# An opening reordered: two row blocks of w_in loaded and multiplied ahead of batch 0's last head pair, seven columns open instead of six

## The chip, the cores and the metric

The kernel runs on one core of one Trainium2 chip. The metric is device microseconds of that core for one launch. Before the change it takes 258.86 us, the median of 3 runs (258.49 to 258.88).

## What is computed

For 8 batches, 8 heads, 576 positions and head size 64, a linear attention is followed by an RMS norm per head, and its output, put side by side over the heads, goes through a two-layer block with a quick GELU:

```python
kv  = einsum('bhsd,bhse->bhde', k, v)
out = einsum('bhsd,bhde->bhse', q, kv)
x   = out / sqrt(mean(out * out, -1) + 1e-6) * g_norm      # then heads side by side: 4608 x 512
h   = x @ w_in                                              # w_in 512 x 2048
g   = h * (1 / (1 + exp(-1.702 * h)))
y   = g @ w_out                                             # w_out 2048 x 512
```

Inputs and output are float32 in memory; the loads cast to float16 and products are summed in float32.

## The kernel before, in words

The 4608 rows are worked in nine tiles of 512: tile t (0 to 7) holds the first 512 positions of batch t, and the ninth the 64 positions left over of each batch. The hidden size 2048 is 16 columns of 128 (`fo`), and the model size 512 is four row blocks of 128 (`ko`); row block c of w_in meets x of head pair c, since two heads of 64 make 128. A hidden column is four TensorE matmuls of 128x512 that add up in one PSUM bank, one for each row block. Below, (k, f) is the matmul of row block k into column f (`Hidden.mm`, line 478).

Tiles 1 to 8 use a seven-product scheme for both layers (lines 589 and 709). Tile 0, with which the program opens, is done plainly: hidden columns at line 478, the second layer at line 822 (`project_all`). Everything is issued in the order in which the code is written (`manual_schedule`), each engine works through its own list, and semaphores are set by the framework.

The opening, lines 860 to 923, works through the four head pairs c of batch 0. For each of them:

- `kv(c)`: 12 small matmuls (line 261) give k'v, and VectorE writes it into `kvb` (line 429);
- `q(c)`: 12 transposes (line 439) turn q, and VectorE copies them to `qT` (line 445);
- `out(c)`: one matmul (line 307) gives `outT`, ScalarE squares it into `sq` (line 325);
- `ss(c)`: one matmul with ones (line 384) sums the squares, ScalarE makes the reciprocal root `rs` (line 386);
- `apply(c)`: VectorE multiplies `outT`, g and `rs` into block c of `xT` (line 394), which is the x of row block c.

`busy(n)` (line 869) issues n matmuls of 128x512 whose result nobody reads. Columns are opened as the x blocks come: before the change six of them, in the order of `COLS`, get row blocks 0 to 2 and then, in one sweep, row block 3 and their activation `gate` (line 487). The ten that are left follow one at a time in `first_columns` (line 804), each with four matmuls and a gate. A column holds a PSUM bank from its first matmul until its gate. There are three pools of banks: `ps_h` (three), `ps_a` (three) and `ps_o` (two).

All loads but pair 0's go through GpSimd's queue (POOL), in the order written: q, k and v of pairs 1 to 3 (line 91, 144 KB each), w_in in pieces (line 180), then w_out (line 206) and batch 1's q, k and v. Eight semaphores serve these loads in turn, so a load is issued only when the one eight places ahead of it has landed.

Of the kernel before, what the change touches and what calls it, by code (L numbers as in the profile page):

```python
# [7 lines left out]
F16 = mybir.dt.float16  # L8
# [4 lines left out]
P = 128  # L13
# [3 lines left out]
def kernel(  # L17
# [12 lines left out]
    B, H, S, D = q.shape  # L30
    DM = H * D
    DFF = moe_w_in.shape[1]
    NPAIR = H // 2
    FO = DFF // P
    KO = DM // P
# [6 lines left out]
    EARLY = 2  # L42
    PE_ = 96
    NJ = S // PE_
    GROUP = 6
    COLS = (0, 1, 2, 3, 8, 9, 10, 11, 4, 5, 6, 12, 13, 7, 14, 15)
    assert PE_ * NJ == S and PE_ % 32 == 0

# [7 lines left out]
    ps_a = ctx.enter_context(tc.tile_pool(name="ps_a", bufs=3, space=bass.MemoryType.PSUM))  # L56
    ps_h = ctx.enter_context(tc.tile_pool(name="ps_h", bufs=3, space=bass.MemoryType.PSUM))
    ps_o = ctx.enter_context(tc.tile_pool(name="ps_o", bufs=2, space=bass.MemoryType.PSUM))
# [31 lines left out]
    def early_load(n, b, c0, c1):  # L90
        nc.gpsimd.dma_start(  # L91
            out=raw[n][0:PE_, c0:c1, :].rearrange("p c (l x) -> p (c l) x", l=2),
            in_=early_src(n, b, c0, c1),
        )
# [84 lines left out]
    def load_w_in(f0, f1, k0=0, k1=KO):  # L179
        nc.gpsimd.dma_start(  # L180
            out=w_in_sb[:, k0:k1, f0 * P : f1 * P],
            in_=moe_w_in[k0 * P : k1 * P, f0 * P : f1 * P].rearrange(
                "(ko ki) f -> ki ko f", ki=P
            ),
        )

    for c in range(1, NPAIR):
        for n in "qkv":
            early_load(n, 0, c, c + 1)
    load_w_in(0, 4, 0, 1)  # L190
    load_w_in(0, 4, 1, 2)
    load_w_in(0, 4, 2, 3)
    load_w_in(8, 10)
    load_w_in(0, 4, 3, KO)
    load_w_in(10, 12)
    load_w_in(4, 8)
    load_w_in(12, FO)

    nc.scalar.preload_act_table_set("abs_reciprocal_sqrt_and_small")
    nc.vector.memset(eps_t, EPS)  # L200
# [220 lines left out]
    class First(Early):  # L421
# [10 lines left out]
                ones2.rearrange("p (l d) -> p l d", l=2),  # L432
            )

        def q(self, c):
            t = ps_h.tile([P, S], F16, name="q0", tag="hT")
            for j in range(NJ):
                for hl in range(2):
                    nc.tensor.transpose(
                        t[hl * D : (hl + 1) * D, j * PE_ : (j + 1) * PE_],  # L440
                        qraw[0:PE_, c, (hl * NJ + j) * D : (hl * NJ + j + 1) * D],
                        ident[0:PE_, 0:PE_],
                    )
            s = attn.tile([P, S], F16, name="qT", tag="qT", bufs=4)
            nc.vector.tensor_copy(s, t)
            self.qT[c] = s
# [340 lines left out]
    def layers(t, units1, units2):  # L787
        hid = d0 if t == 0 else Hidden(t)
        seven = Seven(t, hid.gT) if t else None
        left = hid_seven(t, hid, seven, units1) if t else first_columns(hid, units1)  # L790
        osbs[t] = opool.tile([P, 4, DM], F32, name="osb", tag="osb")
        if t:
            todo = {n: [lambda x=x: seven.sums(*x) for x in xs] for n, xs in plan(t).later.items()}
            for n, us in units2.items():
                todo.setdefault(n, []).extend(us)
            for n, us in left.items():
                todo[n] = us + todo.get(n, [])
            seven.run(todo)
        else:
            project_all(hid.gT, units2)  # L800
        if EARLY <= t < B and t not in HALVED:
            store(t, 0, J)

    def first_columns(hid, units):

        for i, fo in enumerate(COLS):
            if i >= GROUP:
                for ko in range(KO):
                    hid.mm(ko, fo)
                hid.gate(fo)  # L810
            for u in units.get(i, ()):
                u()
# [45 lines left out]
    a0 = First(0)  # L858
# [8 lines left out]
    def busy(n):  # L867
        for _ in range(n):
            nc.tensor.matmul(  # L869
                idle_ps,  # L870
                kvb[1][:, 0, :],
                kvb[1].rearrange("p c r -> p (c r)"),
                start=True,
                stop=True,
            )
# [14 lines left out]
    a0.kv(1)  # L890
    a0.ss(0)
    a0.out(1)
    a0.q(2)
    busy(1)
    a0.kv(2)
    a0.ss(1)
    a0.apply(0)
    a0.out(2)
    a0.q(3)
    a0.apply(1)  # L900
    d0 = Hidden(0)
    busy(3)
    a0.kv(3)
    a0.ss(2)
    a0.apply(2)
    d0.mm(0, 0)
    d0.mm(0, 1)
    a0.out(3)
    d0.mm(0, 2)
    d0.mm(0, 3, ps_a, "att")  # L910
    for fo in range(4):
        d0.mm(1, fo)
        if fo == 1:
            a0.ss(3)
            a0.apply(3)
    for fo in range(4):
        d0.mm(2, fo)
    for fo in COLS[4:GROUP]:
        for ko in range(KO - 1):
            d0.mm(ko, fo, ps_o, "o")  # L920
    for fo in COLS[0:GROUP]:
        d0.mm(KO - 1, fo)
        d0.gate(fo)
# [197 lines left out]
```

## Time and profile before

| what | value |
|---|---|
| median of 3 runs | 258.86 us |
| profiled execution, first to last instruction (span) | 256.5 us |
| median less that span | 2.36 us |
| PE busy / PE clock granted | 98% of the span / 1.000 |
| VectorE, ScalarE, GpSimd busy | 76%, 69%, 23% |
| first hidden matmul of tile 0 | starts at 13.81 us |
| first matmul of the second layer of tile 0 | starts at 28.23 us |

Start times are microseconds from the span's start. A row of the timeline gives start, duration, engine, line, operation, what it writes and reads, how many instructions were merged into the row, and, in brackets, how long the engine had stood idle before it and what ended that. PE is the matmul part of TensorE, PEld its weight loads, DVE VectorE, ACT ScalarE, POOL GpSimd. A matmul's duration holds its way through the array; the next one starts well before it ends, so the pace of a stretch is read from starts, not from durations. The time of a run of the profiled execution itself is not given apart from its span; what the runs take beyond the span is put down as the 2.36 us above.

### The profile page before, as it was taken

How to read it: one execution, taken by the hardware profiler on the slowest of the kernel's cores; microseconds unless marked ns; L12 is line 12 of the kernel's file. 1: busy time of each engine (PE TensorE's matmuls, PEld its weight loads, DVE VectorE, ACT ScalarE, POOL GpSimd, SP SyncE). 2: the span in 40 equal slices, each digit the busy share in tenths (PEclk: the TensorE clock that was granted, in tenths of full speed). 3: DMA queues.
4: the chain of work that ended last, by engine and by line, in shares of the span. 5: the costliest groups of instructions: out<-in, count | busy, mean ns of one | idle time of the engine just before them, and what ended most of it. 6: DMA issues, size and time to landing. Idle time of an engine off the chain costs nothing.

```text
span 256.5 us, 6359 instructions
## 1 busy us (share of the span) xinstructions
PE 250.5 (98%) x2600; PEld 203.8 (79%) x2600; DVE 194.4 (76%) x341; ACT 177.0 (69%) x322; POOL 57.8 (23%) x94
## 2 busy tenths in 40 slices
PE   7899999999999999999999999999999999999994
PEld 2444544788888888888888888888888889888883
DVE  1557585999958895989588867986899687857872
ACT  3469725978759885989598958995798569537800
POOL 8882155404080104301340143000000000000013
PEclk9999999999999999999999999999999999999999
DMA  7999999998999989998999699909500730012005
GB/s 180 189 201 205 205 204 196 191 178 128 165 183 214 118 115 172 216 273 109 211 170 137 87 228 128 177 4 156 184 4 0 93 155 3 0 75 91 3 19 146
DMA packets 68703, 35.33 MB, mean 138 GB/s; under 512 B 37986, under 2 KB 66274, under 8 KB 68418
## 3 DMA queue, kind: packets, MB, share of 16 engines
q0 software_dynamic: 37648, 18.31, 55.4%
q1 hardware_dynamic: 30624, 16.29, 28.7%
q8 instruction: 20, 0.33, 0.6%
q10 hardware_dynamic: 402, 0.33, 0.4%
q14 instruction: 9, 0.07, 0.1%
HBM read 36.70 MB, written 9.44 MB: 180 GB/s over the span
## 4 chain that ended last, share of the span: by engine, by line
PE 94%; DMA 2%; POOL 2%; DVE 0%; issue 0%
PE o L709 38%; PE h L589 38%; PE o L822 5%; PE hT L478 5%; DMA vbuf<-in_v_dram 2%; PE kvp L248 2%; PE outR L337 1%; PE ss L384 1%; POOL qraw L91 1%; PE outT L307 1%; POOL kraw L91 0%; PE q L459 0%; PE kvp L261 0%; PE idle L869 0%; PE kv L261 0%; PE outT L311 0%
## 5 line engine op out<-in xcount | busy, mean ns | idle before, releaser
L566 ACT ACTIVATE gT<-h 128x512 f16<-128x512 f32 x96 | 52.4, 602 | 5.7 <-PE h L589 5.7
L589 PEld LDWEIGHTS <-ws 128*128 128x128 f16 x512 | 50.0, 98 | 6.0
L709 PEld LDWEIGHTS <-gS 128*128 128x128 f16 x512 | 49.0, 98 | 6.2 <-DVE gS L641 0.3
L589 PE MATMUL h<-xS,ws 128*128 128x256 f16 x384 | 52.2, 273 | 0.0
L709 PE MATMUL o<-tw,gS 128*128 128x256 f16 x384 | 45.6, 273 | 0.0
L589 PEld LDWEIGHTS <-w_in_sb 128*128 128x128 f16 x384 | 37.5, 98 | 4.7
L709 PEld LDWEIGHTS <-gT 128*128 128x128 f16 x384 | 37.6, 98 | 4.3
L709 PE MATMUL o<-w_out_sb,gT 128*128 128x256 f16 x256 | 31.4, 273 | 0.0
L589 PE MATMUL h<-xT,w_in_sb 128*128 128x256 f16 x224 | 31.1, 272 | 0.0
L603 DVE TENSOR_TENSOR h<-h,s 128x512 f32<-128x512 f32 x32 | 22.3, 698 | 4.4 <-PE h L589 2.8
L605 DVE TENSOR_TENSOR s<-h,s 128x512 f32<-128x512 f32 x32 | 22.1, 691 | 4.3 <-PE h L589 3.5
L686 DVE TENSOR_TENSOR osb<-o,qf 128x512 f32<-128x512 f32 (+1 forms) x25 | 16.7, 668 | 11.2 <-PE o L709 11.1
L743 POOL DMA_DIRECT2D out_dram<-osb x6 | 3.2, 538 | 93.2 <-DVE osb L686 93.2
L641 DVE TENSOR_TENSOR gS<-gT 128x512 f16<-128x512 f16 (+2 forms) x32 | 21.3, 684 | 0.6 <-ACT gT L566 0.6
L566 ACT ACTIVATE gT<-s 128x512 f16<-128x512 f32 x32 | 19.8, 628 | 2.8 <-DVE s L605 2.8
L589 PE MATMUL h<-xS,w_in_sb 128*128 128x256 f16 x128 | 18.9, 273 | 0.0
L353 DVE TENSOR_REDUCE sum<-sq 128x8 f32<-128x512 f16 x24 | 14.9, 679 | 4.7 <-ACT sq L347 4.7
L995 ACT ACT_TABLE_LOAD x14 | 18.0, 1283 | 0.3
L535 DVE COPY s<-h 128x512 f32<-128x512 f32 x19 | 13.0, 685 | 6.5 <-PE h L589 6.4
L325 ACT ACTIVATE sq<-outT 128x512 f16<-128x512 f32 (+1 forms) x16 | 7.8, 493 | 14.3 <-PE outT L307 8.7
L115 POOL DMA_DIRECT2D kraw<-in_k_dram x7 | 6.0, 855 | 49.1 <-PE kvp L248 32.5
L386 ACT ACTIVATE rs<-ss,eps_t 128x512 f32<-128x512 f32 (+1 forms) x16 | 9.2, 581 | 11.2 <-PE ss L384 11.2
(105 smaller groups left out, 372.2 us busy)
## 6 DMA issues: line engine op xcount, KB each, us to landing
out_dram<-osb SPq DMA_DIRECT2D x8, 512.0 KB, 5.4
kraw<-in_k_dram POOLq DMA_DIRECT2D x5, 512.0 KB, 6.0
vbuf<-in_v_dram POOLq DMA_DIRECT2D x5, 512.0 KB, 10.0
out_dram<-osb SPq DMA_DIRECT2D x2, 1024.0 KB, 4.1
qraw<-in_q_dram POOLq DMA_DIRECT2D x3, 512.0 KB, 11.0
qbuf<-in_q_dram POOLq DMA_DIRECT2D x3, 512.0 KB, 12.8
out_dram<-osb SPq DMA_DIRECT2D x6, 192.0 KB, 6.7
w_in_sb<-in_moe_w_in_dram POOLq DMA_DIRECT2D x2, 512.0 KB, 9.6
```

The source lines that it names most:

```text
L353: nc.vector.tensor_reduce(out=self.sum4[:, j, :], in_=self.o[j][1].rearrange("p (x d) -> p x d", d=D), op=ALU.add, axis=mybir.AxisListType.X,)
L478: nc.tensor.matmul(self.h[fo], w_in_sb[:, ko, fo * P : (fo + 1) * P], self.x[:, ko], start=(ko == 0), stop=(ko == KO - 1),)
L535: (nc.vector.tensor_copy if engine == "D" else nc.scalar.copy)(to, src)
L566: nc.scalar.activation(self.gT[:, to, n * TH : (n + 1) * TH], src, AFT.Gelu_apprx_sigmoid)
L589: nc.tensor.matmul(bank[name][:, a], w, x, start=(p in (1, 5) and a == 0 and k == 0), stop=(k == KH - 1), skip_group_check=True,)
L603: nc.vector.tensor_add(bank["z"], bank["x"], self.s5)
L605: nc.vector.tensor_add(self.s5, bank["x"], self.s5)
L641: op(s[:, n, lo], a, b)
L686: nc.vector.tensor_add(o, ps, self.kept[with_][:, m])
L709: nc.tensor.matmul(o, a, w, start=(p in (1, 2, 5) and i == 0 and (mo == 0 or split)), stop=(i == HF - 1), skip_group_check=True,)
L822: nc.tensor.matmul(os[mo], gT[:, fo, mo * P : (mo + 1) * P], w_out_sb[:, fo, :], start=(fo == 0), stop=(fo == FO - 1),)
L995: u2.setdefault(i, []).append(lambda: f(*args))
```

## The change

**Loads.** The two pieces of w_in for columns 0 to 3, row blocks 0 and 1, are put in front of pair 3's q, k and v on GpSimd's queue. Columns 8 to 11 come in four pieces of one row block each instead of two pieces of two columns each, and columns 4 to 7 and 12 to 15 in two pieces of two row blocks each instead of one. That is 12 loads of w_in where there were 8, of the same bytes.

On GpSimd's list before the change, from pair 2's v on (names are the tiles written and the tensor read, then the shape):

```order
L91 DMA vbuf<-in_v_dram 96x2x384
L91 DMA qraw<-in_q_dram 96x2x384
L91 DMA kraw<-in_k_dram 96x2x384
L91 DMA vbuf<-in_v_dram 96x2x384
L180 DMA w_in_sb<-in_moe_w_in_dram 128x512 x3
L180 DMA w_in_sb<-in_moe_w_in_dram 128x4x256
L180 DMA w_in_sb<-in_moe_w_in_dram 128x512
```

The same place on GpSimd's list after it:

```order
L91 DMA vbuf<-in_v_dram 96x2x384
L180 DMA w_in_sb<-in_moe_w_in_dram 128x512 x2
L91 DMA qraw<-in_q_dram 96x2x384
L91 DMA kraw<-in_k_dram 96x2x384
L91 DMA vbuf<-in_v_dram 96x2x384
L180 DMA w_in_sb<-in_moe_w_in_dram 128x512 x6
L180 DMA w_in_sb<-in_moe_w_in_dram 128x2x512 x4
```

Two loads of w_in have passed pair 3's three loads; the third 128x512 piece, row block 2 of columns 0 to 3, keeps its place as the twelfth load of the queue.

**The opening's order.** x blocks are scaled sooner on VectorE, pair 3's transposes and products move behind the first hidden matmuls on TensorE, the four `busy` matmuls between pairs 1 and 3 go, and a seventh column is opened.

VectorE's list before, between pair 1's and the end of pair 3's work (qT is pair c's turned q, kvb0 its k'v, xT the scaled block):

```order
L429 TENSOR_TENSOR kvb0_87<-kv0_216,ones2_98 128x128
L445 COPY qT_251<-q0_238 128x576
L429 TENSOR_TENSOR kvb0_87<-kv0_254,ones2_98 128x128
L394 SCALAR_TENSOR_TENSOR xT_143<-outT_197,g_col_101,rs_232 128x512
L445 COPY qT_290<-q0_277 128x576
L394 SCALAR_TENSOR_TENSOR xT_143<-outT_234,g_col_101,rs_270 128x512
L429 TENSOR_TENSOR kvb0_87<-kv0_297,ones2_98 128x128
L394 SCALAR_TENSOR_TENSOR xT_143<-outT_273,g_col_101,rs_313 128x512
```

VectorE's list after, same place:

```order
L432 TENSOR_TENSOR kvb0_87<-kv0_220,ones2_98 128x128
L397 SCALAR_TENSOR_TENSOR xT_147<-outT_201,g_col_101,rs_236 128x512
L448 COPY qT_256<-q0_243 128x576
L432 TENSOR_TENSOR kvb0_87<-kv0_262,ones2_98 128x128
L397 SCALAR_TENSOR_TENSOR xT_147<-outT_238,g_col_101,rs_260 128x512
L448 COPY qT_308<-q0_295 128x576
L397 SCALAR_TENSOR_TENSOR xT_147<-outT_281,g_col_101,rs_293 128x512
L432 TENSOR_TENSOR kvb0_87<-kv0_314,ones2_98 128x128
```

Each scaled block has moved one place ahead: block 0 before pair 2's copy of qT, block 1 before pair 3's copy, block 2 before pair 3's k'v.

TensorE's list after, from `ss(1)` on, with the weight loads left out and one row standing for the 12 of pair 2's k'v, pair 3's transposes and pair 3's k'v (hT_277, 279, 286 and 288 are columns 0 to 3):

```order
L387 MATMUL ss_258<-sq_240,ones2_98 128x512
L264 MATMUL kv0_262<-vbuf_96,kraw_94 64x64
L481 MATMUL hT_277<-xT_147,w_in_sb_102 128x512
L481 MATMUL hT_279<-xT_147,w_in_sb_102 128x512
L310 MATMUL outT_281<-qT_256,kvb0_87 128x512
L481 MATMUL hT_286<-xT_147,w_in_sb_102 128x512
L481 MATMUL hT_288<-xT_147,w_in_sb_102 128x512
L387 MATMUL ss_291<-sq_283,ones2_98 128x512
L442 MATMUL q0_295<-ident_97,qraw_95 64x96
L264 MATMUL kv0_314<-vbuf_96,kraw_94 64x64
L310 MATMUL outT_330<-qT_308,kvb0_87 128x512
L387 MATMUL ss_340<-sq_332,ones2_98 128x512
```

Before, all of pair 3's transposes and k'v stood in front of the first hidden matmul; now five hidden matmuls, (0, 0) to (0, 3) and (1, 0), stand in front of its transposes, three more in front of its k'v, and two more in front of `out(3)`.

The diff, whole but for its surrounding lines:

```diff
-    GROUP = 6
+    GROUP, MORE = 7, (9, 10)
...
     for c in range(1, NPAIR):
+        if c == NPAIR - 1:
+            load_w_in(0, 4, 0, 1)
+            load_w_in(0, 4, 1, 2)
         for n in "qkv":
             early_load(n, 0, c, c + 1)
-    load_w_in(0, 4, 0, 1)
-    load_w_in(0, 4, 1, 2)
     load_w_in(0, 4, 2, 3)
-    load_w_in(8, 10)
+    for k0 in range(KO - 1):
+        load_w_in(8, 12, k0, k0 + 1)
     load_w_in(0, 4, 3, KO)
-    load_w_in(10, 12)
-    load_w_in(4, 8)
-    load_w_in(12, FO)
+    load_w_in(8, 12, 3, KO)
+    for f0 in (4, 12):
+        load_w_in(f0, f0 + 4, 0, 2)
+        load_w_in(f0, f0 + 4, 2, KO)
...
-        def q(self, c):
-            t = ps_h.tile([P, S], F16, name="q0", tag="hT")
+        def q(self, c, pool=ps_h, tag="hT"):
+            t = pool.tile([P, S], F16, name="q0", tag=tag)
...
             if i >= GROUP:
+                pool = (ps_o, "o") if i in MORE else (ps_h, "hT")
                 for ko in range(KO):
-                    hid.mm(ko, fo)
+                    hid.mm(ko, fo, *pool)
...
     a0.out(1)
+    a0.apply(0)
     a0.q(2)
-    busy(1)
+    a0.ss(1)
     a0.kv(2)
-    a0.ss(1)
-    a0.apply(0)
-    a0.out(2)
-    a0.q(3)
-    a0.apply(1)
     d0 = Hidden(0)
-    busy(3)
-    a0.kv(3)
-    a0.ss(2)
-    a0.apply(2)
     d0.mm(0, 0)
     d0.mm(0, 1)
-    a0.out(3)
+    a0.out(2)
+    a0.apply(1)
     d0.mm(0, 2)
     d0.mm(0, 3, ps_a, "att")
-    for fo in range(4):
+    d0.mm(1, 0)
+    a0.ss(2)
+    a0.q(3, ps_o, "o")
+    for fo in range(1, 4):
         d0.mm(1, fo)
-        if fo == 1:
-            a0.ss(3)
-            a0.apply(3)
+    a0.apply(2)
+    a0.kv(3)
     for fo in range(4):
         d0.mm(2, fo)
-    for fo in COLS[4:GROUP]:
-        for ko in range(KO - 1):
-            d0.mm(ko, fo, ps_o, "o")
+        if fo == 1:
+            a0.out(3)
+    d0.mm(0, COLS[4], ps_o, "o")
+    d0.mm(0, COLS[5], ps_a, "att")
+    a0.ss(3)
+    a0.apply(3)
+    for ko in range(1, KO - 1):
+        for fo in COLS[4:6]:
+            d0.mm(ko, fo)
+    for ko in range(KO - 1):
+        d0.mm(ko, COLS[6], ps_o, "o")
```

The sweep of row block 3 with the gates now goes over seven columns. The lines of `first_columns` that follow put the tenth and eleventh column (i = 9 and 10) into `ps_o`.

## The prediction, as put on record

> **What bounds the kernel now.** First the page's busy times, then the busy time of each engine over two stretches.
>
> ```profile
> PE 250.5 (98%) x2600; PEld 203.8 (79%) x2600; DVE 194.4 (76%) x341; ACT 177.0 (69%) x322; POOL 57.8 (23%) x94
> ```
>
> ```profile
> 9.77:13.80 4.03, 3.55 (x56) 1.78 (x55) 2.68 (x6) 1.99 (x4) 3.56 (x6) 1.00 1.28 201
> ...
> 13.80:28.20 14.40, 14.40 (x71) 6.51 (x71) 9.37 (x17) 11.53 (x20) 6.65 (x10) 1.00 1.30 203
> ```
>
> The columns are length, then busy time of PE, PEld, DVE, ACT and POOL, the granted clock, the DMA share and GB/s. From 13.80 us on PE has no gap, so what is won or lost ahead of 13.80 moves the end by as much, as long as loads and other engines keep up. The loads run at some 200 GB/s through both stretches: they are the second limit. Next, TensorE's timeline over the opening.
>
> ```profile
> 9.00 0.38 PE L384 MATMUL ss<-sq,ones 128*128 128x512 f16 x1
> 9.45 0.39 PE L307 MATMUL outT<-qT,kvb 128*128 128x512 f16 x1
> 9.77 0.45 PE L439 MATMUL q<-ident,qraw 96*64 96x96 f16 x12
> 10.15 0.39 PE L869 MATMUL idle<-kvb 128*128 128x512 f16 x1
> 10.95 0.38 PE L261 MATMUL kv<-vbuf,kraw 96*64 96x64 f16 x12 [0.42 <-DMA vbuf<-in_v_dram]
> 11.27 0.39 PE L384 MATMUL ss<-sq,ones 128*128 128x512 f16 x1
> 11.72 0.39 PE L307 MATMUL outT<-qT,kvb 128*128 128x512 f16 x1
> 12.04 0.45 PE L439 MATMUL q<-ident,qraw 96*64 96x96 f16 x12
> 12.41 0.82 PE L869 MATMUL idle<-kvb 128*128 128x512 f16 x3
> 13.17 0.38 PE L261 MATMUL kv<-vbuf,kraw 96*64 96x64 f16 x12
> ...
> 13.81 0.61 PE L478 MATMUL hT<-xT,w_in_sb 128*128 128x512 f16 x2
> 14.25 0.38 PE L307 MATMUL outT<-qT,kvb 128*128 128x512 f16 x1
> ...
> 15.33 0.38 PE L384 MATMUL ss<-sq,ones 128*128 128x512 f16 x1
> 15.54 5.79 PE L478 MATMUL hT<-xT,w_in_sb 128*128 128x512 f16 x26
> 21.17 0.28 PE L419 MATMUL outT<-qT,kvb 128*128 128x64 f16 x4
> 21.32 7.08 PE L478 MATMUL hT<-xT,w_in_sb 128*128 128x512 f16 x32
> 28.23 1.24 PE L822 MATMUL o<-w_out_sb,gT 128*128 128x512 f16 x5
> ```
>
> A hidden matmul costs (21.17 - 15.54) / 26 = 0.216 us. Before, 18 of them (row blocks 0 to 2 of six columns) precede (3, 0), which starts at 15.54 + 12 x 0.216 = 18.13. The 46 behind it and the 0.15 us of the four small ones end at 18.13 + 46 x 0.216 + 0.15 = 28.22, the row's 28.23.
>
> **What it removes.** Four idle matmuls, 4 x 0.216 = 0.86 us, and pair 3's transposes (12.04 to 12.41) and k'v no longer stand ahead of (0, 0). All of it can be won only if hidden matmuls can run in the holes. That hangs on two things: when the loads land, and how fast the chain from a product to its scaled block is.
>
> **Loads.** These rows give issues and the time from issue to landing: the chain's row for pair 2's v, then pair 3's v, the first and the third piece of w_in.
>
> ```profile
> 5.28 5.54 DMA vbuf<-in_v_dram
> ...
> 7.14 0.64 POOL L91 DMA_DIRECT2D vbuf<-in_v_dram  x1
> vbuf<-in_v_dram POOLq DMA_DIRECT2D x1, 144.0 KB, 5.9
> 7.76 0.58 POOL L180 DMA_DIRECT2D w_in_sb<-in_moe_w_in_dram  x1
> w_in_sb<-in_moe_w_in_dram POOLq DMA_DIRECT2D x1, 128.0 KB, 6.0
> 9.53 0.53 POOL L180 DMA_DIRECT2D w_in_sb<-in_moe_w_in_dram  x1 [0.64 <-DMA qraw<-in_q_dram]
> w_in_sb<-in_moe_w_in_dram POOLq DMA_DIRECT2D x1, 128.0 KB, 5.4
> ```
>
> So pair 2's v lands at 10.82, pair 3's v at 13.04, w_in's first piece at 13.76 and its third at 14.93. At 200 GB/s a 128 KB piece takes 0.64 us and a 144 KB one 0.74. After the change the two pieces follow pair 2's v: they land at about 11.45 and 12.1, pair 3's q, k and v at 12.8, 13.6 and 14.3, and the third piece at 14.93 as before, because the same bytes precede it. The four pieces of columns 8 to 11 follow at 0.64 us each among the rest: 15.6, 16.2, 16.9 and 18.1, with block 3 of columns 0 to 3 at 17.5. These landings are estimates, and no row shows the new order; if the queue shares bandwidth differently, each may be a piece (0.64 us) earlier or later. I take the middle.
>
> **The chain from `out` to a scaled block.** One row of pair 1's squares, then pair 3's rows and the gates, all before:
>
> ```profile
> 10.00 0.59 ACT L325 ACTIVATE sq<-outT 128x512 f16<-128x512 f32 x1
> ...
> 14.66 0.60 ACT L325 ACTIVATE sq<-outT 128x512 f16<-128x512 f32 x1
> 15.74 0.69 ACT L386 ACTIVATE rs<-ss,eps_t 128x512 f32<-128x512 f32 x1 [0.48 <-PE ss L384]
> 16.47 0.75 DVE L394 SCALAR_TENSOR_TENSOR xT<-outT,g_col,rs 128x512 f16<-128x512 f32 x1 [1.09 <-ACT rs L386]
> 18.56 4.03 ACT L487 ACTIVATE gT<-hT 128x512 f16<-128x512 f32 x8 [0.83 <-PE hT L478]
> ```
>
> From a matmul's start to its reader's start are 0.41 us (14.25 to 14.66, 15.33 to 15.74), sq takes 0.60, rs 0.69 and the scaling 0.75, with 0.04 to 0.07 between engines. From `out` to a usable block that is 3.02 us, when `ss` waits for nothing else.
>
> **The new order, step by step** (PE starts):
>
> - `ss(1)` at 10.65, behind sq(1), which ends at 10.59; `kv(2)` at 10.95 as before, bound by pair 2's v.
> - (0, 0) at 11.50, when the first piece has landed: 0.2 us idle. Block 0 is scaled by 9.00 + 0.41 + 0.69 + 0.04 + 0.75 = 10.89, since it no longer waits behind pair 2's copies. (0, 1) 11.72, `out(2)` 11.93, (0, 2), (0, 3), then (1, 0) at 12.58, for which block 1 is ready at 12.57.
> - `ss(2)` waits for sq until 12.99 (0.2 idle). Transposes 13.20 to 13.58, (1, 1) to (1, 3) to 14.23.
> - `kv(3)` waits for pair 3's v: 14.3 + 0.13 (as at 10.82 to 10.95) = 14.45, to 14.77.
> - (2, 0) waits for the third piece (14.93) and for block 2 (12.99 + 0.41 + 0.69, then behind pair 3's copy to 14.90): 14.98. VectorE scales block 2 ahead of pair 3's k'v, which is written by 15.2, in time for `out(3)` at 15.41.
> - (2, 2), (2, 3), (0, 8), (0, 9), `ss(3)` at 16.49, then four matmuls to 17.57 and, once rs(3) frees a bank at 17.64, three for the seventh column to 18.29.
> - Block 3 is usable at 15.41 + 3.02 = 18.43: (3, 0) starts there.
>
> (3, 0) is thus 0.30 us **later** than before, but 21 hidden matmuls precede it instead of 18, worth 3 x 0.216 = 0.65. The rest is 43 x 0.216 + 0.15 = 9.44, so the second layer starts at 27.87 instead of 28.23: **0.36 us sooner**. Of the 0.86 us of idle matmuls and the 0.42 before `kv(2)`, some 0.9 comes back as waits in the new order. The bounds go with the landings: a piece later each, (2, 0) and all behind it are 0.64 late, a loss of 0.28; a piece earlier each, about 1.0 is won.
>
> **What hides the rest.** Gates follow at 4.03 / 8 = 0.50 us from about 18.43 + 0.43 = 18.86 (the 0.43 as from 18.13 to the first gate at 18.56). The tenth and eleventh column take the banks of the fifth and seventh gate, free at 21.4 and 22.4, and open at 21.8 and 22.65: 0.2 us of cover. If that is gone, the eleventh column waits, by what the gates are late. More loads mean 4 more issues of 0.53 us on POOL, which waits for landings anyway and has seven loads under way at each: nothing. Larger runs in columns 8 to 11 may speed the queue, which only adds cover. Two covers end soonest: batch 1's q and w_out's thirteenth block.
>
> ```profile
> 29.24 1.24 DVE L98 COPY qbuf<-qraw 96x768 f16<-96x768 f16 x4 [1.32 <-DMA qraw<-in_q_dram]
> 29.50 0.56 POOL L206 DMA_DIRECT2D w_out_sb<-in_moe_w_out_dram  x1 [2.21 <-DMA qraw<-in_q_dram]
> w_out_sb<-in_moe_w_out_dram POOLq DMA_DIRECT2D x1, 128.0 KB, 11.4
> 30.50 0.42 PE L459 MATMUL q<-ident,qbuf 96*128 96x96 f16 x6
> 41.59 0.39 PE L822 MATMUL o<-w_out_sb,gT 128*128 128x512 f16 x1
> ```
>
> The first copy of qbuf is done by 29.6 and read at 30.50: 0.9 of cover. The block lands at 40.9 and is read at 41.59: 0.69. Both exceed 0.36, so the gain is kept; a gain of over 0.7 would be cut there unless the queue is faster too. Behind that PE stays full, as the same instructions follow in the same order.
>
> **Sum.** 256.5 - 0.36 = 256.1 us of span; with the 2.36 us that the median holds beyond the span, 258.5 us.
>
> **Rivals.**
>
> *Loads land sooner* (0.25). Half a piece, 0.3 us, earlier for all takes the waits at (0, 0), `kv(3)` and (2, 0) with it: a gain of 0.36 + 0.3 = 0.66, 258.2 us, still under the cover. For it: the queue's rate is 0.59 us a piece between w_in's first and third. Against it: block 2 is then next, at 14.95.
>
> *Given back* (0.13). A bank wait at the tenth or eleventh column, or the loads above, eats the 0.36: 258.9 us.
>
> *Half pace* (0.09), on the slower side. At the program's start idle matmuls come every 0.42 us at first. The stretch's busy times (columns as above), then the first and the seventh start:
>
> ```profile
> 1.28:5.97 4.69, 4.40 (x14) 1.49 (x14) 0.56 (x1) 2.12 (x2) 4.59 (x11) 1.00 0.91 227
> ```
>
> ```profile
> 1.28 0.61 PE L869 MATMUL idle<-kvb 128*128 128x512 f16 x1 [1.28 <-DVE one_t L202]
> ...
> 3.81 0.98 PE L869 MATMUL idle<-kvb 128*128 128x512 f16 x2
> ```
>
> From 1.28 to 3.81 six start, 2.53 - 6 x 0.216 = 1.23 us more than at full pace, though the granted clock reads 1.00: PE gets its pace after it has been busy. The four idle matmuls removed kept it busy: 3.55 of 4.03 us, a share of 0.88; in the new order I count 3.8 of the 5.2 us from 9.77 to 14.98, a share of 0.73. If this falls under what keeps the pace, one such stretch costs 1.23: 258.86 - 0.36 + 1.23 = 259.7. It decides from the point where the busy share falls under that of any stretch that kept the pace, so somewhere below 0.88. Against it: the holes are 0.2 us, and PE kept its pace behind the 0.42 before `kv(2)`. The Trainium skill, "TensorE: Matmul & The Clock Gate", under "Why this matters for your kernels", asks for no PE gaps over some 3 us between bursts; by that rule the 0.2 us holes cost nothing and the time stays 258.5. The 0.42 us hole before `kv(2)`, with the pace kept behind it, agrees. The same page, "Part 4: PE-mode transpose", says that transposes do not count as busy in the same way, which would lower the share further; no run here shows it.
>
> *The pieces do not land sooner* (0.05), because eight loads share the engines: (0, 0) starts at 13.81, and 21 hidden matmuls, four others, the transposes and k'v (6.1 us) bring (3, 0) to 19.9, 1.1 us after the 18.78 that would be even: 260.0.
>
> **How the numbers follow.** The sum holds at 0.48: 258.5 us. A measurement of this kernel can tell about 0.2%, 0.52 us, from no change: under 258.34 is faster, over 259.38 slower. Faster is the first rival and a fifth of the forecast's chance: 0.35. Slower is the third and fourth: 0.14. The rest is the same: 0.51. The range takes the landings' bounds, 257.9 to 259.1, and leaves out the two slow rivals and a little above the first.
>
> **What would show it.** In the changed profile (0, 0) should start near 11.5, (2, 0) near 15.0, (3, 0) near 18.4 and the second layer near 27.9, PE full behind. A start of (0, 0) past 12, a hole at the tenth or eleventh column, a pace of 0.43 us in the opening, or a wait for qbuf or w_out behind 28 us would make it wrong.

## The result, and the profile after

The changed kernel takes **259.1 us** (median of 15 runs, 258.73 to 259.99), the kernel before 258.52 us on the same chip (15 runs, 258.02 to 259.46). The ratio is 1.0025, with a 95% interval from 1.0014 to 1.0036: slower by a quarter of a per cent, where 258.5 us and no measurable change, or a gain, were forecast. A second comparison, on another occasion, gave 258.92 against 258.68 us, ratio 1.0016 [1.0001, 1.0030]. The profiled execution has a span of 257.3 us. Two runs of the kernel before in later comparisons, of 262.81 and 1397.38 us, were slow ones and are in no ratio below.

First the page's line of busy times after the change:

```profile
PE 250.9 (97%) x2596; PEld 203.7 (79%) x2596; DVE 194.2 (75%) x341; ACT 176.8 (69%) x322; POOL 59.7 (23%) x98
```

TensorE has four instructions fewer, the idle matmuls, and is busy 0.4 us longer; the span is 0.8 us longer. Its timeline over the new opening says where (start, duration, and in brackets the idle time with what ended it):

```profile
11.09 0.38 PE L387 MATMUL ss<-sq,ones 128*128 128x512 f16 x1 [0.43 <-ACT sq L328]
...
11.80 0.61 PE L481 MATMUL hT<-xT,w_in_sb 128*128 128x512 f16 x2
...
13.30 0.38 PE L387 MATMUL ss<-sq,ones 128*128 128x512 f16 x1
...
14.78 0.38 PE L264 MATMUL kv<-vbuf,kraw 96*64 96x64 f16 x12
15.54 0.61 PE L481 MATMUL hT<-xT,w_in_sb 128*128 128x512 f16 x2 [0.39 <-DVE kvb L432]
...
17.28 4.26 PE L481 MATMUL hT<-xT,w_in_sb 128*128 128x512 f16 x18
...
21.49 7.07 PE L481 MATMUL hT<-xT,w_in_sb 128*128 128x512 f16 x32
```

The instructions stand as the change put them, at full pace (32 matmuls from 21.49 to 28.40, 0.216 us each). But (0, 0) starts at 11.80, not 11.50, in an execution whose first products came 0.45 us later than in the one the forecast read; (2, 0) at 15.54, not 14.98; and the second layer at 28.40, not 27.87. The row at 15.54 names VectorE, but the third piece of w_in, which (2, 0) reads, lands only then. Its issue, and the time from issue to landing:

```profile
9.37 0.56 POOL L180 DMA_DIRECT2D w_in_sb<-in_moe_w_in_dram  x1
w_in_sb<-in_moe_w_in_dram POOLq DMA_DIRECT2D x1, 128.0 KB, 6.1
```

That is 15.47; "14.93 as before" was forecast. The loads' own rate says why. The last column is GB/s, from 9.75 to 11.25 us, of the kernel before and then of the changed one:

```profile
9.75:11.25 1.50, 1.08 (x26) 0.70 (x25) 0.46 (x1) 0.84 (x2) 1.21 (x3) 1.00 1.30 197
```

```profile
9.75:11.25 1.50, 1.00 (x15) 0.50 (x14) 0.76 (x2) 1.17 (x2) 1.08 (x3) 1.00 1.22 160
```

Before, pair 2's and pair 3's loads run in this stretch; after, the rest of pair 2's and then the moved pieces of w_in do, and the rate falls. One more loss stands far behind the opening in this profile, a wait for batch 4's last piece of v:

```profile
115.14 0.32 PE L251 MATMUL kvp<-vbuf,kraw 128*64 128x64 f16 x8 [0.43 <-DMA vbuf<-in_v_dram]
```

Every run's time was 1.72 to 1.85 us above its own span (258.66 for a span of 256.9, say). The forecast put down 2.36 us: the execution profiled before was itself some 0.6 us quicker than the median that the forecast set it against.

### The profile page after: what moved, and what is told of

Its sections match the earlier page's. It is cut to its first block, busy times and chain, and to the rows that moved or that the text cites. A ratio compares the mean times of both kernels' runs of the same rounds, so it can differ in the third digit from the quotient of the medians.

```text
span 257.3 us, 6356 instructions
## 1 busy us (share of the span) xinstructions
PE 250.9 (97%) x2596; PEld 203.7 (79%) x2596; DVE 194.2 (75%) x341; ACT 176.8 (69%) x322; POOL 59.7 (23%) x98
## 4 chain that ended last, share of the span: by engine, by line
PE 91%; DMA 6%; DVE 1%; ACT 1%; POOL 0%; issue 0%
PE o L712 38%; PE h L592 33%; DMA vbuf<-in_v_dram 6%; PE o L826 5%; PE hT L481 5%; PE idle L873 2%; PE kvp L251 2%; PE outR L340 1%; PE ss L387 1%; PE outT L310 1%; ACT sq L328 0%; PE q L462 0%; PE kvp L264 0%; PE q L442 0%; PE outT L314 0%; ACT rs L389 0%
## 5 line engine op out<-in xcount | busy, mean ns | idle before, releaser
L538 ACT COPY h<-h 128x512 f32<-128x512 f32 x27 | 15.4, 577 | 2.1 <-PE h L592 1.8
```

Source lines behind the costliest of these rows:

```text
L538: (nc.vector.tensor_copy if engine == "D" else nc.scalar.copy)(to, src)
```

## The experiments

At first, theory A was that the loss is the wait at 115 us, theory B that the new opening is slower in itself. After four runs A was dropped, and two theories on the opening were left: L, loads that land late, each used just as it lands; and B, the new order, apart from its loads. L1 and L2, M1 and M2 are told where they come up. The table gives what each profile's readings rest on: the start of pair 0's k'v, `kv(0)`, which stands behind pair 0's transposes and is the first product of loaded k and v, at the same place in both orders; the start of the second layer; the span.

| kernel | time us (runs) | ratio to before | kv(0) | second layer | from one to the other | span |
|---|---|---|---|---|---|---|
| before, profile of the forecast | | | 6.98 | 28.23 | 21.25 | 256.5 |
| before_again | 258.66 (1) | | 7.57 | 28.67 | 21.10 | 256.9 |
| before_third | 258.07 (1) | | 7.43 | 28.09 | 20.66 | 256.3 |
| changed | 259.10 (15) | 1.0025 [1.0014, 1.0036] | 7.43 | 28.40 | 20.97 | 257.3 |
| after_again | 259.71 (1) | | 7.29 | 29.69 | 22.40 | 257.9 |
| after_third | 258.92 (12) | 1.0016 [1.0001, 1.0030] | 6.96 | 29.20 | 22.24 | 257.8 |
| no_split | 259.67 (6) | 1.0044 [1.0029, 1.0058] | 7.58 | 29.54 | 21.96 | 257.8 |
| loads_only | 261.09 (7) | 1.0090 [1.0053, 1.0127] | 7.57 | 31.04 | 23.47 | 259.3 |
| order_only | 261.32 (4) | 1.0092 [1.0060, 1.0124] | 7.33 | 31.06 | 23.73 | 259.3 |
| split_only | 258.79 (11) | 1.0003 [0.9992, 1.0014] | 7.17 | 28.96 | 21.79 | 257.3 |
| after_no_pair3 | 258.24 (11) | 0.9984 [0.9970, 0.9998] | 7.42 | 28.05 | 20.63 | 256.3 |
| before_no_pair3 | 258.24 (10) | 0.9980 [0.9969, 0.9991] | 7.54 | 28.14 | 20.60 | 256.4 |
| one_moved | 259.54 (12) | 1.0026 [1.0008, 1.0044] | 7.30 | 28.40 | 21.10 | 256.9 |
| one_piece | 258.81 (10) | 1.0011 [0.9993, 1.0029] | 7.69 | 29.06 | 21.37 | 257.4 |
| contig_two | 258.94 (11) | 1.0018 [1.0000, 1.0036] | 7.01 | 28.31 | 21.30 | 256.7 |
| contig_all | 258.42 (11) | 0.9993 [0.9982, 1.0003] | 7.18 | 27.81 | 20.63 | 256.1 |
| contig_all_2 | 258.34 (11) | 0.9994 [0.9984, 1.0004] | 7.53 | 28.15 | 20.62 | 256.4 |
| contig_all_3 | 258.27 (12) | 0.9989 [0.9978, 0.9999] | 7.31 | 27.94 | 20.63 | 256.2 |
| before_contig | 258.41 (11) | 0.9993 [0.9982, 1.0004] | 7.52 | 28.47 | 20.95 | 256.8 |
| before_contig_2 | 258.41 (11) | 0.9995 [0.9987, 1.0004] | 7.49 | 28.10 | 20.61 | 256.5 |

In 17 of the 20 profiles the span is 228.2 to 228.4 us more than the start of the second layer, whatever the opening; the exceptions are the changed kernel's first profile (228.9, the wait at 115 us), after_third (228.6) and one_moved (228.5). So the opening sets the time.

### Both kernels again

No edit.

> The kernel before, unchanged, for a second profile. Theory A (the loss lies behind the opening, in a wait for batch 4's last piece of v at about 114 us, whose landing is close to its need whichever kernel runs): the second layer of tile 0 starts at 28.2 to 28.4 us, and the stage from 101 to 127 us shows either no gap or one of up to 0.5 us; span 256.3 to 257.0. Theory B (the new opening itself is slower): no gap behind 28 us, span within 0.2 us of 256.5.

> The changed kernel, unchanged, for a second profile. Theory A: the wait at 114 us is there again or, if it is absent, the span is 0.4 to 0.6 us shorter than the first profile's 257.3; the second layer of tile 0 starts between 27.8 (when the idle matmuls at the start reach full pace early) and 28.4 us (when late). Theory B: the second layer starts later than 28.4 us, with no wait behind it, and the span is 257.0 or more.

`before_again` fell outside both brackets: its second layer starts at 28.67 us, with 0.17 us of waiting for a gate ahead of 21.75 us, and its span is 256.9 us, without a gap behind 29 us. The changed kernel's second profile has no wait at 115 us and is slower than the first. Its timeline, from pair 3's k'v on:

```profile
15.30 0.38 PE L264 MATMUL kv<-vbuf,kraw 96*64 96x64 f16 x12 [0.39 <-DMA vbuf<-in_v_dram]
15.87 0.60 PE L481 MATMUL hT<-xT,w_in_sb 128*128 128x512 f16 x2 [0.20 <-DMA w_in_sb<-in_moe_w_in_dram]
...
22.61 2.76 PE L481 MATMUL hT<-xT,w_in_sb 128*128 128x512 f16 x12 [0.20 <-DMA w_in_sb<-in_moe_w_in_dram]
25.79 4.06 PE L481 MATMUL hT<-xT,w_in_sb 128*128 128x512 f16 x18 [0.42 <-DMA w_in_sb<-in_moe_w_in_dram]
29.69 0.59 PE L826 MATMUL o<-w_out_sb,gT 128*128 128x512 f16 x2
```

Four waits for loads, all ahead of 28 us, and the second layer at 29.69. Theory A falls: the wait at 115 us is in no other profile. One profile alone had put the loss in the wrong place.

### The change in halves

`loads_only` is the changed kernel with the order of before put back in the opening:

```diff
...
-    a0.apply(0)
     a0.q(2)
-    a0.ss(1)
+    busy(1)
     a0.kv(2)
+    a0.ss(1)
+    a0.apply(0)
+    a0.out(2)
+    a0.q(3)
+    a0.apply(1)
     d0 = Hidden(0)
+    busy(3)
...
```

`no_split` is the changed kernel with the later pieces of w_in as they were:

```diff
-    for k0 in range(KO - 1):
-        load_w_in(8, 12, k0, k0 + 1)
+    load_w_in(8, 10)
     load_w_in(0, 4, 3, KO)
-    load_w_in(8, 12, 3, KO)
-    for f0 in (4, 12):
-        load_w_in(f0, f0 + 4, 0, 2)
-        load_w_in(f0, f0 + 4, 2, KO)
+    load_w_in(10, 12)
+    load_w_in(4, 8)
+    load_w_in(12, FO)
```

> The kernel before with the changed kernel's loads, its matmul order kept. Pair 3's loads land some 1.3 us later, and pair 3's transposes stand ahead of every hidden matmul, so the first hidden matmul starts some 1.2 us later, at 15.0; from there on a share of it is lost for good. Theory A with the loads as cause: about 1 us from the opening and a further 0.4 from the wait at 114 us, 260.0 or more. Theory B (opening order as cause): about 259.6, with no wait at 114 us.

> The changed kernel with w_in's later pieces as before (8 loads instead of 12), the two first pieces still in front of pair 3. Theory A, if the number of loads shifts the later loads on the queue: no wait at 114 us, second layer at 27.8 to 28.4, time 258.0 to 258.5, up to 0.2% under the kernel before. Theory A, if the wait is a matter of the opening's timing alone: 259.0 as the changed kernel. Theory B (opening): 259.0, with the second layer at 28.4 or later.

`no_split` is above every bracket, and its ratio of 1.0044 is above the changed kernel's, though the two intervals touch: the fifth column's weights are waited for.

```profile
17.55 0.60 PE L479 MATMUL hT<-xT,w_in_sb 128*128 128x512 f16 x2 [0.71 <-DMA w_in_sb<-in_moe_w_in_dram]
```

So in this profile the new order needs the split by row blocks. `loads_only` lost more, but not for its loads alone; its first hidden matmul starts at 16.27 us, where 15.0 was expected. Its timeline, then its busy times, where the column ahead of the last two is the granted clock:

```profile
13.51 0.58 PE L442 MATMUL q<-ident,qraw 96*64 96x96 f16 x12 [1.29 <-DMA qraw<-in_q_dram]
14.02 1.46 PE L872 MATMUL idle<-kvb 128*128 128x512 f16 x3
```

```profile
13.80:16.30 2.50, 2.50 (x25) 0.93 (x22) 1.41 (x3) 0.00 (x0) 1.88 (x3) 0.50 1.23 198
```

Pair 3's q now lands behind the moved pieces, TensorE stands idle for 1.29 us, and then works at half its clock (0.50 from 14 to 17 us as well).

Not every execution did so. The mean granted clock of a whole run tells them apart: three of the seven runs read 1.000 and took 259.43 to 259.94 us, four read 0.987 to 0.993 and took 261.09 to 262.54 (3.5 us at 0.50 in a span of 259 us make 0.993).

`order_only` is the counterpart, the changed order with all loads as before:

```diff
-        if c == NPAIR - 1:
-            load_w_in(0, 4, 0, 1)
-            load_w_in(0, 4, 1, 2)
         for n in "qkv":
             early_load(n, 0, c, c + 1)
+    load_w_in(0, 4, 0, 1)
+    load_w_in(0, 4, 1, 2)
...
```

> The changed order with the loads of before. Theory L: (0, 0) waits for the first piece, which lands at 13.8 to 14.0 as before, with TensorE idle for some 2.3 us ahead of it; the fourth rival's sum gives 260.0 us at full pace. TensorE was at half pace behind a hole of 1.29 us in the run with the loads alone, so here it should be at half pace for 1 to 3 us behind the hole: 260 to 261.5 us. Theory B: about the same as the changed kernel, 259 to 259.7.

```profile
13.65 1.03 PE L478 MATMUL hT<-xT,w_in_sb 128*128 128x512 f16 x2 [1.97 <-DMA w_in_sb<-in_moe_w_in_dram]
```

```profile
13.65:16.60 2.95, 2.95 (x9) 0.92 (x11) 0.00 (x0) 0.60 (x1) 1.06 (x2) 0.55 1.36 197
```

As expected: the first piece lands at 13.64, the hole is 1.97 us, and a clock of 0.55 over the 2.95 us behind it. Of its four runs, one read a clock of 0.999 and took 259.83 us; the others read 0.987 to 0.993 and took 261.06 to 262.09. So each half alone costs 0.9%, and still 0.3 to 0.5% in the runs that kept the clock; both together cost less. `split_only` is the kernel before with the later pieces split (no_split's diff turned round) and nothing moved:

> The kernel before with columns 4 to 15 of w_in in more and smaller loads (eight pieces of whole row blocks or halves where there were four of columns), nothing moved. Theory L: same bytes, no dip of the rate at 10 to 12 us since no piece of w_in runs there, and all later pieces still land ahead of their use: within 0.1% of before, 258.3 to 258.9. If the number of loads were what costs, the rate would fall under 190 GB/s somewhere from 14 to 24 us and the time would be 259.1 or above.

In the median it costs nothing (1.0003 [0.9992, 1.0014]), so the number of loads by itself isn't what costs. Its one profile, though, shows what both theories had left out, a wait for a piece of columns 8 to 11 while the rate is low:

```profile
17.58 4.52 PE L480 MATMUL hT<-xT,w_in_sb 128*128 128x512 f16 x19 [0.57 <-DMA w_in_sb<-in_moe_w_in_dram]
```

```profile
16.00:18.00 2.00, 1.40 (x6) 0.37 (x4) 1.63 (x3) 1.51 (x2) 0.89 (x2) 1.00 1.19 160
```

### Without pair 3's loads

In both kernels pair 3's three loads are left out, and pair 3 reads pair 2's q, k and v (so its values are another pair's). The changed kernel's edit, of which the kernel before's differs only in how the loads are left out:

```diff
-        for n in "qkv":
+        for n in "qkv" if c < NPAIR - 1 else "":
...
-            self.kv_product(t, c)
+            self.kv_product(t, min(c, 2))
...
```

> The changed kernel without pair 3's three loads (432 KB); pair 3 reads pair 2's q, k and v, so its values are another pair's. Theory L (the loss is loads that land later than forecast, each used as it lands): 432 KB at 200 GB/s are 2.1 us, so the third piece lands at 13.4 to 13.8 instead of 15.5, pair 3's k'v and (2, 0) wait for no load, the second layer starts at 27.6 to 28.0 and the time is 258.0 to 258.5 us, at or under the kernel before. Theory B (the new order is slower in itself, by its engines or its pace): the second layer still starts at 28.4 or later and the time stays at 259.1 or above.

> The kernel before without pair 3's three loads, as a control; pair 3's values are again pair 2's. Theory L: the kernel before used no load behind pair 2's v just as it landed, so nothing is won: second layer at 28.2 to 28.7, time within 0.1% of before (258.3 to 258.8). Theory B: the same. If it were faster by 0.5 us or more, the loads bound the kernel before as well, and theory L's cover is wrong.

Both take 258.24 us. Pair 0's k'v and the second layer of the changed order, then of the old one:

```profile
7.42 0.38 PE L264 MATMUL kv<-vbuf,kraw 96*64 96x64 f16 x12
...
28.05 1.24 PE L826 MATMUL o<-w_out_sb,gT 128*128 128x512 f16 x5
```

```profile
7.54 0.38 PE L261 MATMUL kv<-vbuf,kraw 96*64 96x64 f16 x12
...
28.14 1.24 PE L822 MATMUL o<-w_out_sb,gT 128*128 128x512 f16 x5
```

Theory L holds for the changed kernel: 0.7 to 0.9 us go with the waits, and the second layer starts only 0.05 us past its bracket. But the control, which L expected to stay within 0.1% of before, gained 0.2%, and its second layer came 0.06 us ahead of the bracket: the kernel before loses to its loads too, in some executions (in the forecast's profile 0.42 us ahead of pair 2's k'v). And with no load waited for, the two orders are **equal**: 20.63 and 20.60 us from kv(0) to the second layer.

### More profiles, and two other ways to load

`one_moved` puts only the first piece ahead of pair 3, and has TensorE take up pair 3 ahead of row block 1:

```diff
-            load_w_in(0, 4, 1, 2)
...
+    load_w_in(0, 4, 1, 2)
     load_w_in(0, 4, 2, 3)
...
+    a0.kv(3)
     d0.mm(1, 0)
+    a0.out(3)
+    a0.apply(2)
...
```

`one_piece` loads the two moved pieces as one:

```diff
-            load_w_in(0, 4, 0, 1)
-            load_w_in(0, 4, 1, 2)
+            load_w_in(0, 4, 0, 2)
```

> The changed kernel unchanged, for a third profile and more runs. Theory L (late landings that differ from one execution to the next): w_in's first piece lands at 11.4 to 11.9 us but the second, pair 3's three and the third land 0.3 to 0.9 us later than forecast, the rate falls under 170 GB/s somewhere from 10 to 12 us, the second layer starts between 28.2 and 29.7 and the time is 259.1 to 259.7. Theory B (the order in itself): the loads keep 195 GB/s or more from 10 to 24 us and the time is the same.

> The kernel before unchanged, for a third profile. Theory L: it uses no load just as it lands but pair 2's v, so with the usual differences in the loads the second layer still starts at 28.2 to 28.7 and the span is 256.3 to 257.2.

> The changed kernel with only the first piece of w_in ahead of pair 3; the second goes behind pair 3's v, and TensorE works pair 3 as soon as its loads land, ahead of row block 1. Theory L: pair 3's v lands 0.64 us sooner than in the changed kernel, at 13.7 to 14.3, out(3) starts at 14.6 to 15.1, so (3, 0) at 17.6 to 18.2, with 18 to 19 hidden matmuls ahead of it. The pieces of row blocks 1 and 2 are waited for less, and the second layer starts at 27.7 to 28.4: 257.9 to 258.7 us, at or under the kernel before. Theory B: the order costs what it cost before, 259.1 or more.

> The changed kernel with the two moved pieces as one load of 256 KB. If the rate falls at 10 to 12 us because of how many loads there are or where one ends, it should now stay at 195 GB/s, pair 3's v lands at 14.3 and the time falls to 258.5 to 258.9, although (0, 0) then waits for the whole load until 12.2. If the rate falls as these addresses are read at this time, whatever the load (my guess), it stays at 100 to 150 GB/s for a microsecond, (0, 0) starts at 12.3 to 12.9 and the time is 259.3 to 260.

after_third behaves as L says in the main: 154 GB/s from 9.75 to 11.25 us, the third piece at 15.60, waits of 0.78, 0.18 and 0.35 us for w_in, second layer at 29.20; the first piece, at 12.0, is later than L's bracket, and the median of 258.92 us lies under it. A wait of 0.27 us for a block of w_out follows at 38.11 us. The kernel before shows no wait for a load in its third profile, whose second layer, at 28.09, is 0.11 us ahead of the bracket. `one_moved` didn't win what L expected of it: its median is 259.54 us, and even in its profiled run, one of its quickest (258.67 us), pair 3's v landed at 14.17, and holes stay in front of pair 3's k'v and of row block 1,

```profile
14.34 0.38 PE L264 MATMUL kv<-vbuf,kraw 96*64 96x64 f16 x12 [0.42 <-DMA vbuf<-in_v_dram]
14.89 0.39 PE L481 MATMUL hT<-xT,w_in_sb 128*128 128x512 f16 x1 [0.17 <-DMA w_in_sb<-in_moe_w_in_dram]
```

so this other order doesn't repair it. In `one_piece` the rate falls to 166 GB/s all the same, so it isn't the two loads in place of one that make it fall; its median of 258.81 us isn't told from before or from the changed kernel, and the 259.3 that I guessed was too high.

### The source in memory

Still open was why the rate falls. A piece of w_in, 128 rows by 512 columns, is 128 runs of 2 KB with 6 KB between them; 128 rows of w_out are one block of 256 KB. `contig_all` reads all pieces from w_out, in the same order, sizes and shapes (the weights are other numbers); `contig_two` only the two moved ones; `before_contig` is the control, in which the pieces of 256 columns are half rows of w_out, runs of 1 KB with 1 KB between. The edit of `contig_all`:

```diff
-            in_=moe_w_in[k0 * P : k1 * P, f0 * P : f1 * P].rearrange(
+            in_=moe_w_out[(f0 + k0) * P : (f0 + k1) * P, :].rearrange(
```

> The changed kernel with every piece of w_in read from w_out instead, in the same order, sizes and shapes: a piece of 128 rows by 512 columns is then one contiguous block of 256 KB in memory and not 128 runs of 2 KB with 6 KB between them. The weights are thus other numbers. If the rate falls because of how w_in lies in memory (theory L1), it stays at 190 GB/s or more from 10 to 24 us, pair 3's v lands at 14.3 and the third piece at 14.9, the second layer starts at 27.8 to 28.1 and the time is 258.0 to 258.5. If it falls because of the place in the stream or the time (theory L2), the rate still falls to 110 to 150 GB/s for a microsecond at 10 to 11 us and the time is 258.9 to 259.5.

> The changed kernel with only the two moved pieces read from w_out, contiguous; the others come from w_in as before. Theory L1: no fall of the rate at 10 to 11 us, pair 3's v lands at 14.3 and (2, 0) starts at 15.0 to 15.2; a fall can come later, where columns 8 to 15 are read; time 258.3 to 258.9. Theory L2: the fall at 10 to 11 us is there as in the changed kernel, pair 3's v at 14.6 to 15.2 and the time 258.9 to 259.5.

> The control: the kernel before with all pieces of w_in read from w_out (the 512-column ones contiguous). It has cover, so by both theories the second layer starts at 28.1 to 28.7. L1: some of its slower executions go, 258.2 to 258.6. L2: as before, 258.5 to 258.8.

L2 falls: place in the stream and time are the same, and the rate no longer falls. L1 holds as far as it was tested: the fall goes with what is read. The runs of 2 KB and the tensor were exchanged together, though, and no run reads w_in in one block or w_out in runs of 2 KB at this time, so that the layout is the reason is likely and not shown. Rates of contig_all and then of contig_two:

```profile
9.75:11.25 1.50, 1.07 (x20) 0.50 (x21) 0.91 (x2) 1.04 (x2) 0.85 (x2) 1.00 1.26 197
16.00:18.00 2.00, 2.00 (x10) 0.87 (x9) 0.39 (x1) 1.50 (x3) 1.79 (x3) 1.00 1.24 204
```

```profile
9.75:11.25 1.50, 1.07 (x26) 0.65 (x25) 1.05 (x2) 1.03 (x3) 0.99 (x2) 1.00 1.25 200
16.00:18.00 2.00, 1.98 (x10) 0.64 (x9) 0.00 (x0) 1.21 (x2) 1.43 (x3) 1.00 1.15 164
```

Where contiguous pieces are read, 197 to 204; where contig_two goes back to w_in, 164, and its time stays at 258.94, at the edge between L1's bracket and L2's (pair 2's v was 0.2 us late in its profile, and all behind it: (2, 0) starts at 15.26, past L1's 15.2). Over all profiles in which pieces of w_in are read from 9.75 to 11.25 us, that stretch ran at 106 to 177 GB/s in 9 of 9 (160, 152, 154, 132, 106, 117, 136, 166, 177), and at 191 to 200 in 4 of 4 with contiguous pieces. With the loads mended, contig_all's timeline comes out at the forecast's times from (0, 0) on:

```profile
11.46 0.61 PE L481 MATMUL hT<-xT,w_in_sb 128*128 128x512 f16 x2
...
13.00 0.38 PE L387 MATMUL ss<-sq,ones 128*128 128x512 f16 x1
...
14.44 0.38 PE L264 MATMUL kv<-vbuf,kraw 96*64 96x64 f16 x12
14.96 0.59 PE L481 MATMUL hT<-xT,w_in_sb 128*128 128x512 f16 x2
...
27.81 1.24 PE L826 MATMUL o<-w_out_sb,gT 128*128 128x512 f16 x5
```

The forecast had these at 11.50, 12.99, 14.45, 14.98 and 27.87, and its third piece at 14.93; here it lands at 14.83. That the times agree is luck in part: this execution's kv(0) starts at 7.18, 0.20 us later than the forecast's, and none of the waits for loads that the forecast put ahead of (0, 0), `kv(3)` and (2, 0) is there. Yet the median of 258.42 us equals the control's 258.41. Where the gain went was the last question: M1, the median execution loses it in its opening, or M2, it is given back behind it.

> The changed kernel with all of w_in read from w_out, again (the weights are other numbers). Its profile had the second layer at 27.81 us and a span of 256.1, but its 11 runs had a median of 256.6. If the median execution loses in its opening (M1), a second profile shows an opening that starts later or loads that land later: pair 2's v at 10.9 or later, or waits for loads, with the second layer at 27.9 to 28.6 and the span 228.3 us more than that. If what was won is given back behind it (M2), the second layer starts at 27.8 to 28.0 and the span is 228.6 us or more behind it.

> The same once more, for a third profile; the same two outcomes, M1 and M2, with the same numbers.

> The control again: the kernel before with all of w_in read from w_out. By M1 and M2 the second layer at 28.1 to 28.7, the span 228.2 to 228.4 us behind it. With the runs before it the difference of the two orders over contiguous pieces can be told to some 0.1%: by the forecast the changed order is 0.36 us (0.14%) faster; if it isn't, the order itself is worth nothing.

M1, but by the start and not by the loads. contig_all_2, and then before_contig_2:

```profile
7.53 0.38 PE L264 MATMUL kv<-vbuf,kraw 96*64 96x64 f16 x12
...
28.15 1.03 PE L826 MATMUL o<-w_out_sb,gT 128*128 128x512 f16 x4
```

```profile
7.49 0.38 PE L262 MATMUL kv<-vbuf,kraw 96*64 96x64 f16 x12
...
28.10 1.24 PE L823 MATMUL o<-w_out_sb,gT 128*128 128x512 f16 x5
```

No load is waited for in either, and both orders need 20.6 us from kv(0) on; so did contig_all and contig_all_3 (before_contig, which waited 0.27 us for pair 2's v, needed 20.95). In all, 34 runs of the changed order over contiguous pieces have a median of 258.32 us and 22 of the old order 258.41: of the 0.36 us of the forecast the medians show 0.1, and the way from kv(0) on shows nothing.

Nothing here beats the kernel before with all of its loads: the weights of w_in come as they are, so contiguous pieces are not to be had, and the versions that keep the loads (one_moved, one_piece, split_only) are at or above it.

## Why the prediction was wrong, by its own steps

- **The landings**, the step that failed: "the third piece at 14.93 as before, because the same bytes precede it", by 200 GB/s for whatever is read. The rate depends on what is read when. In the three profiles of the changed kernel the third piece landed at 15.47, 15.83 and 15.60, 0.54 to 0.90 us late, and later pieces were late again in two of them. From kv(0) to the second layer they took 20.97, 22.40 and 22.24 us, against 20.62 to 20.63 with contiguous pieces. The text had named a piece later (0.64 us) as a bound and priced it at a loss of 0.28 us, which is about the measured 0.24 to 0.58, but took "the middle" between a piece later and a piece earlier. The rows gave little ground for the earlier end: the queue ran at 201 and 203 GB/s already. Between the same order with contiguous pieces (258.32 us) and the changed kernel (259.10 and 258.92) lie 0.6 to 0.8 us, on different occasions: that is this term, measured.
- **The gain of 0.36 us**, mis-sized. It was worked out against one execution, whose kv(0) started at 6.98, so early that TensorE then waited 0.42 us for pair 2's v. The forecast's new order has no such wait, and that is nearly all of its gain. The 2.36 us that the sum adds to the span hide the same thing: 1.72 to 1.85 of them are there in every run, and the rest is how much quicker that execution was than the median. In executions that start at 7.4 to 7.5 (before_third, before_contig_2) the old order doesn't wait there either, and the holes that the forecast itself counted in the new order, ahead of ss(1), ss(2) and (2, 0), take up the 0.86 us of the removed idle matmuls: 20.60 to 20.66 against 20.62 to 20.63 us. The base was thus one that most executions don't share, and in the others the order wins nothing.
- **The chain from `out` to a scaled block**: right, 15.39 to 18.41 us from `out(3)` to (3, 0) in contig_all, where 3.02 was forecast. The order of waits: not as forecast. With the loads mended the starts from (0, 0) to `kv(3)` are within 0.11 us of the forecast's and those from (2, 0) on within 0.06, but `ss(1)` and `kv(2)` start 0.20 later (10.85, 11.15), and no load is waited for. The starts hang on kv(0): in contig_all_2, where that starts 0.35 us later, (2, 0) starts 0.35 later too, at 15.31, though its third piece lands sooner, at 14.7.
- **More loads cost nothing**: right in the median for `split_only`; that the pieces of columns 8 to 11 have little cover was not listed, and `no_split` (0.71 us at the fifth column) and `split_only` (0.57) show waits for them. Of the covers of loads, those named were all behind 28 us.
- **What is behind 28 us**: right for the second profile of the changed kernel, not for all. qbuf was not waited for, but a block of w_out was for 0.27 us at 38.11 in after_third, and batch 4's v for 0.43 at 115 us in the first profile, each in one of three.
- **The rivals.** "Loads land sooner" had the sign wrong. "Given back" (258.9 us) came nearest, but by the loads of w_in in the opening, and not by a bank; of what it named, only the wait for w_out came, in one profile. "Half pace" didn't come in the changed kernel's profiles, whose longest hole of 0.78 us kept the pace (one of its runs, of 259.80 us, read a mean clock of 0.993), but came where a hole was 1.29 us (`loads_only`) or 1.97 us (`order_only`). The busy share that the forecast set its point by doesn't tell them apart: from 9.77 to 14.98 us `one_moved` kept the pace with 3.87 of 5.21 us busy, and `loads_only` lost it with 3.78. The forecast's own 0.73 also counted matmuls at 0.216 us, while the 0.88 it was set against counts the rows' busy time; by that measure the changed kernel's first profile reads 4.69 of 5.21, or 0.90. Whether the length of one hole decides, or the share of another stretch, the runs don't settle. "The pieces do not land sooner" was priced at 260.0 us; as an experiment (`order_only`) the one run that kept the clock took 259.83 us, and the median is 261.3, the rest being the half pace.
- **The chances**: slower had 0.14, all of it half pace and no landing at all; a landing one piece late should have carried more, since every load of the new order was to be used as it lands.

Open stays why the kernel before reads the same pieces of w_in, from 13 to 15 us, at 191 to 201 GB/s, and the later ones mostly too (one profile of three falls to 183 GB/s from 16 to 18 us), so that the layout can't be the whole reason. What else is under way at 10 to 11 us, or in the queue, wasn't varied.

## What to carry to other kernels

An order that uses each load just as it lands turns every slow landing into a hole of the bounding engine; before moving work ahead, ask what cover each load has left, and price the landing one piece late as the likely case and not as the end of the range. Compare two orders from an early instruction that stands at the same place in both, over several profiles: a wait that one profile shows can be a matter of when that execution happened to start. Idle instructions that go win nothing when the same chain then leaves holes of the same length.

## What the runs showed of the hardware

- **Reads of w_in in runs of 2 KB with a pitch of 8 KB**, from 9.75 to 11.25 us: the stretch ran at 106 to 177 GB/s, and at 191 to 200 with contiguous blocks of w_out of the same size, although the same strided reads ran at 191 to 201 from 13 to 15 us in the kernel before. The Trainium skill, "DMA: Bandwidth & Descriptors", under "Latency and other measured facts", reports slower copies for large power-of-two row pitches (207 GB/s at 512 KiB, 164 at 2 MiB, 103 at 4 MiB). The loss here came at a far smaller pitch, 8 KB; no run here tried other pitches, so that the pitch is its cause is not shown.
- **TensorE's half pace behind a hole**: behind 1.29 us of idle time in an opening where TensorE had been partly busy, the clock column read 0.50 for 2.5 us. By the runs' mean clocks it came in four of seven executions of that kernel; how long the hole was in the other three isn't known. The rule of the Trainium skill, "TensorE: Matmul & The Clock Gate", under "Why this matters for your kernels", which the forecast used, allows gaps of about 3 us; here the measurement decides. The longest hole with the pace kept behind it was 0.91 us, ahead of pair 0's k'v in `one_piece`.
- **The length of the start differs between executions of one program.** The twelve idle matmuls at the program's start, first in contig_all_3 and then in contig_all_2:

```profile
1.28 4.05 PE L873 MATMUL idle<-kvb 128*128 128x512 f16 x12 [1.28 <-DVE one_t L205]
```

```profile
1.28 5.30 PE L873 MATMUL idle<-kvb 128*128 128x512 f16 x12 [1.28 <-DVE one_t L205]
```

  The second never left half pace in them. With the loads of pair 0 and their copies this puts kv(0) anywhere from 6.96 to 7.69 us, 0.7 us of difference between executions whose code is the same up to there, and twice what the change was forecast to win.
